# Making kv of two batches together, with each remainder tile's o right behind a kv, in a linear-attention and MLP kernel

## The chip, the cores and the metric

The kernel runs on one core of a Trainium2 chip. The metric is the device time of one execution in microseconds (us). Five engines work side by side and tell each other through semaphores: TensorE (matmuls; the profile writes PE, and PEld for its weight loads), VectorE (DVE), ScalarE (ACT), GpSimd (POOL) and SyncE (SP). In this kernel SP issues transposing transfers and stores, and POOL issues the loads that cast from float32 to bfloat16.

## The reference

All sizes are fixed: 8 batches, 8 heads, 576 positions, head size 64, model size 512, hidden size 2048.

```python
kv = np.einsum('bhsd,bhse->bhde', k, v)
out = np.einsum('bhsd,bhde->bhse', q, kv)
rms = np.sqrt(np.mean(out * out, axis=-1, keepdims=True) + 1e-06)
attn = out / rms * g_norm
x = attn.transpose(0, 2, 1, 3).reshape(B, S, H * D)
mu = np.mean(x, axis=-1, keepdims=True)
var = np.mean((x - mu) ** 2, axis=-1, keepdims=True)
xn = (x - mu) / np.sqrt(var + 1e-06) * g_ln
result = x + np.maximum(xn @ w_ch1, 0.0) @ w_ch2
```

The attention has no softmax: for each head a 64 x 64 matrix kv is made from k and v, and q is multiplied by it. Then come a norm per head, a layer norm over 512 columns, and two large matmuls with a ReLU between.

## The kernel before

**Tiles.** A batch's 576 positions are cut into four main tiles of 128 positions and a rest of 64. The rests of two neighbouring batches make one remainder tile: rem 1 holds those of batches 0 and 1, rem 3 of 2 and 3, rem 5 of 4 and 5, rem 7 of 6 and 7. The four remainder tiles form a block of their own, `"rem"`, which the MLP handles last.

**kv.** `kv_of(b)` makes kv of one batch: 40 matmuls with 64 weight columns each, for the head pairs alternately into the lower and the upper half of the array's columns. Two copies on ScalarE take it from PSUM into `kv_pack[b % 4]`. Batches 0 and 1 have code of their own near the start, the first with 64 rows as well.

**q.** `turn_q_dma(b)` copies q on VectorE into another order (`q_p`, line 203) and has SP transpose it by a transfer (`qt`, line 205).

**A tile** has four steps, recorded by `plan_tile`. `first`: `o` on TensorE (line 271: q times kv), its squares on ScalarE (277), their sum per head on VectorE (298). `second`: root (ACT, 308), reciprocal (315), `y` (303), `x` (322, 326) and `xc` (332) on VectorE. `third`: the variance on ScalarE (340). `fourth`: the transpose of `xc` into `xT_blk`, for batches from 2 on by a transfer on SP (352). A main tile's o is 4 matmuls with 128 weight columns, a remainder tile's o is 8 with 64, since each half of its rows has a kv of its own.

**The MLP** is the main stream: `mm1` (line 413), ReLU on ScalarE (416), `mm2` (429), `finish` on VectorE (434, writes `o_sb`), and two stores on SP (447, 448). It goes batch by batch, the remainder block last.

**The order is written by hand.** `mm1` and `mm2` call `tick()` after every few matmuls; each tick is a slot. From batch 3 on, batch b has slots 32 b to 32 b + 31: 16 of `mm1`, 16 of `mm2`, in each of them 4 matmuls of 512 columns. `at(slot, fn)` puts a function into a slot. All that a slot holds is recorded, in the order of its numbers, ahead of that slot's matmuls:

```python
    def tick():
        for _, fn in sorted(agenda.pop(clock[0], []), key=lambda e: e[0]):
            fn()
        clock[0] += 1
```

Every engine runs what is recorded for it strictly in this order; only the semaphores decide when. So a slot's number says where work stands in each queue and not when it starts.

**Slots before.** kv of batches 1, 2 and 3 in slots 22, 36 and 56; kv of 4 in 84, of 5 in 115, of 6 in 147, of 7 in 179. Remainder tiles: o in 62, 82, 146 and 210, with `second` two slots later. q of batch 3 in 56.7, of batch 4 in 84.7.

**Loads.** k, v and q each have two buffers (`NB = 2`), chosen by the batch's number. `load_batch(b, *after)` (lines 96 to 101) issues six transfers on POOL, two halves each for k, v and q. Ahead of them it copies one element of each tile in `after` into `gate`: POOL waits with the loads until that tile is there. Batch 4 waits for the transposed q of batch 3 and the last tile's `xT_blk` of batch 2, later batches for the transposed q of the batch before.

**PSUM.** `ps_out` has two buffers for o, `ps_m` one for kv and small transposes, `ps1` three for `mm1`, `ps2` two for `mm2`.

Of the kernel before, what the change touches and what calls it, by code (L numbers as in the profile page):

```python
# [14 lines left out]
def kernel(  # L15
# [11 lines left out]
    nc = tc.nc  # L27
    f32 = mybir.dt.float32
# [5 lines left out]
    B, H, S, D = q.shape  # L34
# [3 lines left out]
    nK = Dm // 128  # L38
    nDe = Dh // 128
    HP = H // 2  # L40
# [3 lines left out]
    J, JJ, JP = 4, 5, 9  # L44
    S_LO = 64 * JJ
    EPS = 1e-6
    NB = 2
# [8 lines left out]
    ps_m = ctx.enter_context(tc.psum_pool(name="ps_m", bufs=1))  # L56
# [15 lines left out]
    q_in = [consts.tile([128, H, JJ, D], bf16, name=f"q_in{i}") for i in range(NB)]  # L72
    k_in = [consts.tile([128, H, JJ, D], bf16, name=f"k_in{i}") for i in range(NB)]
    v_in = [consts.tile([128, H, JJ, D], bf16, name=f"v_in{i}") for i in range(NB)]
    kv_g = consts.tile([128, HP, 128], bf16)
    kv_pack = [consts.tile([128, HP, 128], bf16, name=f"kv_pack{i}") for i in range(4)]
# [9 lines left out]
    def lo(t, b, h0=0, h1=H):  # L86
        return t[b, h0:h1, :S_LO, :].rearrange("h (p j) d -> p h j d", j=JJ)

    def up(t, b, h0=0, h1=H):
        return t[b, h0:h1, S_LO:, :].rearrange("h (p j) d -> p h j d", j=J)  # L90

    def load(dst, t, b, h0=0, h1=H):
        nc.gpsimd.dma_start(dst[:64, h0:h1], lo(t, b, h0, h1))
        nc.gpsimd.dma_start(dst[64:, h0:h1, :J], up(t, b, h0, h1))

    def load_batch(b, *after):
        for element in after:
            nc.gpsimd.tensor_copy(gate, element)  # L98
        load(k_in[b % NB], k, b)
        load(v_in[b % NB], v, b)  # L100
        load(q_in[b % NB], q, b)

    def load_w1(c):
        n = Dh // 4
# [60 lines left out]
    qts, held, blks, rstds, m1s, q_ps = {}, {}, {}, {}, {}, {}  # L165
# [35 lines left out]
    def turn_q_dma(b):  # L201
        q_p = kv_in.tile([128, JJ, H, D], bf16, tag="qp", bufs=2)
        nc.vector.tensor_copy(q_p.rearrange("p j h d -> p h j d"), q_in[b % NB])
        q_t = qt_pool.tile([128, JJ, HP, 128], bf16, tag="qt", name="qt")
        nc.sync.dma_start_transpose(  # L205
            q_t.rearrange("p j hp t -> p (j hp) t"), q_p.rearrange("p j h d -> p (j h d)"))
        qts[b] = q_t
# [28 lines left out]
            nc.vector.tensor_mul(kv_g[D:, self.hps, D:], self.odd[D:], g[D:])  # L236
            del self.even, self.odd

    def kv_of(b):
        kv_ps = ps_m.tile([128, HP, D], f32, tag="misc", name="kv_ps")  # L240
        kvp = held[b] = kv_pack[b % 4]
        for hp in range(HP):
            for j in range(JJ):
                for hh in range(2):
                    h = 2 * hp + hh
                    nc.tensor.matmul(kv_ps[hh * D:hh * D + D, hp, :],  # L246
                                     lhsT=k_in[b % NB][:, h, j, :], rhs=v_in[b % NB][:, h, j, :],
                                     start=(j == 0), stop=(j == JJ - 1))
        nc.scalar.copy(kvp[:D, :, :D], kv_ps[:D])  # L249
        nc.scalar.copy(kvp[D:, :, D:], kv_ps[D:])  # L250

    def new_block(n, bufs):
        x_blk = xpool.tile([128, 4, Dm], f32, tag=f"x{n}", bufs=bufs, name="x_blk")
        st_blk = xpool.tile([128, 3, 4], f32, tag=f"st{n}", bufs=bufs, name="st_blk")
        xT_blk = xpool.tile([128, nK, 512], bf16, tag=f"xT{n}", bufs=bufs, name="xT_blk")
        return x_blk, st_blk, xT_blk
# [98 lines left out]
    def main_tile(b, j, pool=None, tag="ops"):  # L355
        q_t, kvp = qts[b], held[b]
        if b not in blks:
            blks[b] = new_block("main", 3)
        return Tile([(slice(0, 128), lambda hp: q_t[:, j, hp, :], kvp)], blks[b], j, pool, tag)

    def rem_tile(b):
        mms = []
        for half, bb in enumerate((b - 1, b)):
            qt, kp = qts.pop(bb), held.pop(bb)
            mms.append((slice(half * 64, (half + 1) * 64),
                        lambda hp, qt=qt: qt[:, J, hp, :64], kp))
        if "rem" not in blks:
            blks["rem"] = new_block("rem", 1)
        return Tile(mms, blks["rem"], b // 2)

    def plan_tile(s, make, turn_at, on_pe):
        box = []

        def first():
            t = make()
            box.append(t)
            t.o()
            t.sq()
            t.red()

        def second():
            t = box[0]
            t.y()
            t.x()
            t.xc()

        def third():
            box[0].var()

        def fourth():  # L390
            box[0].turn(on_pe)

        at(s, first)
        at(s + 2, second)
        at(s + 6, third)
        at(turn_at, fourth)

    def m1_of(b):
# [20 lines left out]
    def rstd_of(b):  # L419
        rstd = work.tile([128, 4], f32, tag="rstd", bufs=3, name="rstd")  # L420
        nc.scalar.activation(rstd, blks[b][1][:, 2, :], func=AF.Sqrt, scale=1.0 / Dm, bias=eps_sb)  # L421
        nc.vector.reciprocal(rstd, rstd)  # L422
        rstds[b] = rstd
# [45 lines left out]
    def at(slot, fn):  # L469
        agenda.setdefault(int(slot), []).append((slot, fn))  # L470
# [119 lines left out]
    def next_loads():  # L590
        nc.gpsimd.memset(k_in[0][64:, :, J], 0.0)
        nc.gpsimd.memset(v_in[0][64:, :, J], 0.0)
        load_batch(2)

    at(1, before_1)
    at(2, before_2)
    at(5, lambda: t[2].turn(True))
    at(5.1, before_5)
    at(9.5, next_loads)
    at(11, lambda: t[3].turn(True))  # L600
    for i in range(4):
# [17 lines left out]
    at(14.5, q_start)  # L619
    at(19, q_turns)  # L620
    at(22, lambda: kv_of(1))
    for j, s, tn in ((0, 24, 30), (1, 27, 34), (2, 31, 38), (3, 35, 42)):
        plan_tile(s, lambda j=j: main_tile(1, j), tn, True)
    at(46, lambda: rstd_of(1))

    at(36, lambda: kv_of(2))
    at(36.9, lambda: turn_q_dma(2))
    for j, s, tn in ((0, 45, 51), (1, 49, 55), (2, 53, 61), (3, 57.5, 64)):
        plan_tile(s, lambda j=j: main_tile(2, j), tn, False)
    plan_tile(62, lambda: rem_tile(1), 69, False)  # L630
    at(78, lambda: rstd_of(2))

    for b in range(3, B):
        s = 32 * b
        at(47 if b == 3 else s - 60,
           lambda b=b: load_batch(b, qts[b - 1][:1, J, HP - 1, 127:],
                                  *([blks[2][2][:1, nK - 1, 511:]] if b == 4 else [])))
        d = -41 if b == 3 else -45
        at(s + d + (1 if b < 5 else 0), lambda b=b: kv_of(b))
        at(s + d + 1.7, lambda b=b: turn_q_dma(b))  # L640
        for j in range(J):
            o = s + d + (11 if b == 3 else 13) + 5 * j
            plan_tile(o, lambda b=b, j=j: main_tile(b, j), o + 6, False)
        if b % 2:
            plan_tile(s - 14, lambda b=b: rem_tile(b), s - 8, False)
        at(s + 14, lambda b=b: rstd_of(b))
    at(32 * B + 14, lambda: rstd_of("rem"))


# [56 lines left out]
```

## Time and profile before

| What | us |
|---|---|
| Median of 3 runs (lowest, highest) | 291.13 (290.49, 291.29) |
| The profiled execution | 290.6 |
| Its span, first to last instruction | 288.8 |
| Large matmuls, lines 413 and 429, busy | 131.6 and 129.1 |
| The o of tiles, line 271, busy | 13.7 |
| kv of batches 1 to 7, line 246, busy | 5.8 |

Most matmuls have 512 columns. They overlap, so that the mean of one (379 ns) is longer than the distance from one start to the next. The page's second part shows the span in 40 equal slices, each digit a tenth of busy time:

```profile
PE   7889999999999999999999999999999999999994
PEld 3579756995479644444444444444444444444444
DVE  5774119938897783764376935762578200220022
ACT  3477844985379733872288318921893066016400
POOL 8522510041005004100500032000000000000000
PEclk9999999999999999999999999999999999999999
DMA  7999999979788959996994189947203410230033
```

One slice is 7.2 us. TensorE is busy all along, VectorE is nearly full in some slices between 58 and 108 us, and the DMA engines have full slices wherever loads run. The clock that TensorE was granted is full throughout.

The DMA issues of the page tell the sizes of the transfers and the median time from issue to landing:

```profile
out_dram<-o_sb SPq DMA_DIRECT2D x70, 128.0 KB, 2.4
...
q_in<-in_q_dram POOLq DMA_DIRECT2D x7, 320.0 KB, 12.3
k_in<-in_k_dram POOLq DMA_DIRECT2D x7, 320.0 KB, 6.0
v_in<-in_v_dram POOLq DMA_DIRECT2D x7, 320.0 KB, 8.6
```

A half of a tensor is 320 or 256 KB as it is written, in bfloat16.

### The profile page before, as it was taken

To read this page: it belongs to the slowest core of one execution; us is meant where nothing else is said; L and a number is where in the kernel's file an instruction comes from. 1 tells how busy PE (TensorE), PEld (TensorE's weight loads), DVE (VectorE), ACT (ScalarE), POOL (GpSimd) and SP (SyncE) were. 2 spreads that over 40 slices of the span, in tenths; PEclk is the share of its full clock that TensorE was granted. 3 is DMA by queue.
4 is the path that set the end of the run, shared out by engine and by line. 5 is a ranking of instruction groups with operands and counts; after the bars stand their busy time and mean duration, and the time that the engine had idled before them with its cause. 6 is when DMAs were issued, how large, how long until landed. Compare 5 with 4: busy or idle time off the path is not lost.

```text
span 288.8 us, 5753 instructions
## 1 busy us (share of the span) xinstructions
PE 280.9 (97%) x2295; PEld 157.9 (55%) x2295; DVE 149.8 (52%) x331; ACT 153.2 (53%) x333; POOL 41.0 (14%) x69
## 2 busy tenths in 40 slices
PE   7889999999999999999999999999999999999994
PEld 3579756995479644444444444444444444444444
DVE  5774119938897783764376935762578200220022
ACT  3477844985379733872288318921893066016400
POOL 8522510041005004100500032000000000000000
PEclk9999999999999999999999999999999999999999
DMA  7999999979788959996994189947203410230033
GB/s 214 199 206 205 198 190 195 214 112 193 138 173 101 194 108 157 202 159 120 157 217 68 39 152 219 155 84 149 56 18 64 101 36 0 48 81 19 0 73 75
DMA packets 67546, 36.76 MB, mean 127 GB/s; under 512 B 35516, under 2 KB 62524, under 8 KB 67520
## 3 DMA queue, kind: packets, MB, share of 16 engines
q0 software_dynamic: 28528, 17.76, 43.8%
q1 hardware_dynamic: 38480, 17.91, 31.2%
q10 hardware_dynamic: 512, 0.72, 0.7%
q8 instruction: 18, 0.29, 0.4%
q14 instruction: 8, 0.07, 0.1%
HBM read 36.71 MB, written 9.44 MB: 160 GB/s over the span
## 4 chain that ended last, share of the span: by engine, by line
PE 85%; DMA 5%; DVE 5%; ACT 2%; issue 1%; SPq 1%; DVEq 0%; POOLq 0%
PE p L413 41%; PE p L429 37%; PE o_ps L271 2%; DMA v_in<-in_v_dram 2%; DMA qt<-q_p 2%; PE kv_ps L246 2%; DMA xT_blk<-xc 1%; DVE ss L298 1%; ACT m L416 1%; DVE x_blk L322 1%; DVE y L303 1%; DVE o_sb L434 1%; PE p L198 1%; SPq L205 1%; ACT rms L308 0%
## 5 line engine op out<-in xcount | busy, mean ns | idle before, releaser
L413 PE MATMUL p<-xT_blk,w_sb 128*128 128x128 bf16 (+2 forms) x1024 | 131.6, 286 | 0.6 <-DMA xT_blk<-xc 0.2
L429 PE MATMUL p<-w_sb,m 128*128 128x512 bf16 (+2 forms) x608 | 129.1, 368 | 0.0
L416 ACT ACTIVATE m<-p 128x512 bf16<-128x512 f32 x144 | 85.2, 596 | 43.0 <-PE p L413 40.5
L413 PEld LDWEIGHTS <-w_sb 128*128 128x128 bf16 x1024 | 78.7, 98 | 44.9 <-issue 1.5
L429 PEld LDWEIGHTS <-m 128*128 128x128 bf16 x608 | 57.0, 98 | 62.0
L434 DVE SCALAR_TENSOR_TENSOR o_sb<-p,rstd,x_blk 128x512 f32<-128x512 f32 (+2 forms) x38 | 27.3, 720 | 52.2 <-PE p L429 41.2
L277 ACT ACTIVATE sq<-o_ps 128x512 f32<-128x512 f32 x35 | 20.9, 596 | 41.7 <-PE o_ps L271 41.7
L298 DVE TENSOR_REDUCE ss<-sq 128x8 f32<-128x512 f32 x35 | 23.7, 678 | 13.0 <-ACT sq L277 12.9
L340 ACT ACTIVATE dev<-x_blk,st_blk 128x512 f32<-128x512 f32 x36 | 25.7, 714 | 6.2 <-DVE st_blk L326 6.1
L332 DVE SCALAR_TENSOR_TENSOR xc<-x_blk,st_blk,g_ln_sb 128x512 bf16<-128x512 f32 x34 | 25.6, 752 | 1.2
L303 DVE TENSOR_TENSOR y<-o_ps,inv 128x512 f32<-128x512 f32 x33 | 22.8, 692 | 3.4 <-PE p L413 0.5
L322 DVE SCALAR_TENSOR_TENSOR x_blk<-y,g_norm_sb 128x512 f32<-128x512 f32 x33 | 22.8, 692 | 1.1
L315 DVE RECIPROCAL inv<-rms 128x8 f32<-128x8 f32 x36 | 7.2, 201 | 23.0 <-ACT rms L308 23.0
L422 DVE RECIPROCAL rstd<-rstd 128x4 f32<-128x4 f32 x9 | 1.6, 175 | 31.2 <-ACT rstd L421 31.1
L308 ACT ACTIVATE rms<-ss,eps_sb 128x8 f32<-128x8 f32 x36 | 10.7, 296 | 11.5 <-DVE ss L298 11.4
L98 POOL COPY gate<-qt 1x1 bf16<-1x1 bf16 x5 | 0.9, 177 | 106.4 <-DMA qt<-q_p 106.4
L271 PEld LDWEIGHTS <-qt 128*128 128x128 bf16 (+1 forms) x156 | 10.2, 100 | 8.1 <-issue 1.7
L271 PE MATMUL o_ps<-kv_pack,qt 128*128 128x128 bf16 (+1 forms) x156 | 13.7, 220 | 0.2
L198 PE MATMUL p<-fill_sb 128*128 128x512 bf16 x27 | 8.0, 448 | 1.2 <-DVE eps_sb L137 1.2
L340 ACT ACTIVATION_READ_ACCUMULATOR dev<-x_blk,st_blk 128x1 f32 x36 | 6.8, 189 | 0.0
L249 ACT CAST kv_pack<-kv_ps 64x256 bf16<-64x256 f32 x7 | 2.6, 366 | 7.7 <-PE kv_ps L246 7.7
L246 PEld LDWEIGHTS <-k_in 128*64 128x64 bf16 x280 | 5.0, 112 | 2.6 <-issue 2.5
(80 smaller groups left out, 110.5 us busy)
## 6 DMA issues: line engine op xcount, KB each, us to landing
out_dram<-o_sb SPq DMA_DIRECT2D x70, 128.0 KB, 2.4
w_sb<-in_moe_w_ch_dram POOLq DMA_DIRECT2D x8, 512.0 KB, 15.2
q_in<-in_q_dram POOLq DMA_DIRECT2D x7, 320.0 KB, 12.3
k_in<-in_k_dram POOLq DMA_DIRECT2D x7, 320.0 KB, 6.0
v_in<-in_v_dram POOLq DMA_DIRECT2D x7, 320.0 KB, 8.6
q_in<-in_q_dram POOLq DMA_DIRECT2D x8, 256.0 KB, 12.3
k_in<-in_k_dram POOLq DMA_DIRECT2D x7, 256.0 KB, 6.7
v_in<-in_v_dram POOLq DMA_DIRECT2D x7, 256.0 KB, 10.6
```

The source lines that it names most:

```text
L198: nc.tensor.matmul(p1, lhsT=fill_sb[:, :128], rhs=fill_sb, start=True, stop=True)
L271: nc.tensor.matmul(flat[rows, hp * 128:(hp + 1) * 128], lhsT=lhsT_of(hp), rhs=kvp[:, hp, :], start=True, stop=True)
L277: nc.scalar.activation(self.sq_t, self.o_ps, func=AF.Square)
L298: nc.vector.tensor_reduce(self.ss, self.sq_t, axis=AX.X, op=ALU.add)
L303: nc.vector.tensor_mul(self.y_t, self.o_ps, self.inv().to_broadcast([128, H, D]))
L322: nc.vector.scalar_tensor_tensor(x_blk[:, ts].rearrange("p (h d) -> p h d", h=H), in0=self.y_t, scalar=1.0, in1=g_norm_sb.to_broadcast([12 ...
L332: nc.vector.scalar_tensor_tensor(self.xc_t, in0=x_blk[:, self.ts], scalar=st[:, 1, self.ts:self.ts + 1], in1=g_ln_sb, op0=ALU.add, op1=ALU ...
L340: nc.scalar.activation(dev, x_blk[:, ts], func=AF.Square, bias=st[:, 1, ts:ts + 1], accum_out=st[:, 2, ts:ts + 1])
L413: nc.tensor.matmul(p1[:, i, :], lhsT=w1_sb[:, kk, de * 128:(de + 1) * 128], rhs=blk[2][:, kk, sl], start=(kk == 0), stop=(kk == nK - 1))
L416: nc.scalar.activation(m1[:, de0:de0 + per, sl], p1, func=AF.Relu)
L429: nc.tensor.matmul(p2[:, c0:c1], lhsT=m1s[b][:, de, ts * 128:(ts + 1) * 128], rhs=w2_sb[:, de, c0:c1], start=(de == 0), stop=(de == nDe - 1))
L434: nc.vector.scalar_tensor_tensor(o_sb[:, c0:c1], in0=p2[:, c0:c1], scalar=rstds[b][:, ts:ts + 1], in1=blks[b][0][:, ts, c0:c1], op0=ALU.mu ...
```

## The change

`kv_of` takes one batch or several. For two it makes 80 matmuls in a row into one PSUM tile of twice the size, and then four copies. It is called for (3), (4, 5) and (6, 7) in slots 56, 93 and 147. Right behind it, in the same slot, stands the o of a remainder tile: rem 1, rem 3 and rem 5. `plan_tile` has a new argument `x_at`, the slot of `second`. Rem 7 stays in slot 210.

The loads follow: `load_batches` takes a list of tensors. Behind the gate that let in k, v and q of batch 4 there stand now q, k and v of 4 and k and v of 5; the later gates let in q of one batch and k and v of the next. The order is q first.

Batch 3's tiles are planned 4.7 slots apart instead of 5, batch 4's q in slot 86.4 instead of 84.7, and batch 4's tiles from 97 in steps of 4.75 instead of from 96 in steps of 5. From batch 5 on, q and the main tiles stay in their slots.

```diff
-    def load_batch(b, *after):
+    def load_batches(what, *after):
         for element in after:
             nc.gpsimd.tensor_copy(gate, element)
-        load(k_in[b % NB], k, b)
-        load(v_in[b % NB], v, b)
-        load(q_in[b % NB], q, b)
+        tensors = {"k": (k_in, k), "v": (v_in, v), "q": (q_in, q)}
+        for name, b in what:
+            dst, src = tensors[name]
+            load(dst[b % NB], src, b)
...
-    def kv_of(b):
-        kv_ps = ps_m.tile([128, HP, D], f32, tag="misc", name="kv_ps")
-        kvp = held[b] = kv_pack[b % 4]
-        for hp in range(HP):
-            for j in range(JJ):
-                for hh in range(2):
-                    h = 2 * hp + hh
-                    nc.tensor.matmul(kv_ps[hh * D:hh * D + D, hp, :],
-                                     lhsT=k_in[b % NB][:, h, j, :], rhs=v_in[b % NB][:, h, j, :],
-                                     start=(j == 0), stop=(j == JJ - 1))
-        nc.scalar.copy(kvp[:D, :, :D], kv_ps[:D])
-        nc.scalar.copy(kvp[D:, :, D:], kv_ps[D:])
+    def kv_of(*bs):
+        kv_ps = ps_m.tile([128, len(bs), HP, D], f32, tag="misc", name="kv_ps")
+        for i, b in enumerate(bs):
+            for hp in range(HP):
+                for j in range(JJ):
+                    for hh in range(2):
+                        h = 2 * hp + hh
+                        nc.tensor.matmul(
+                            kv_ps[hh * D:hh * D + D, i, hp, :], lhsT=k_in[b % NB][:, h, j, :],
+                            rhs=v_in[b % NB][:, h, j, :], start=(j == 0), stop=(j == JJ - 1))
+        for i, b in enumerate(bs):
+            kvp = held[b] = kv_pack[b % 4]
+            nc.scalar.copy(kvp[:D, :, :D], kv_ps[:D, i])
+            nc.scalar.copy(kvp[D:, :, D:], kv_ps[D:, i])
...
-        at(s + 2, second)
-        at(s + 6, third)
+        at(x_at or s + 2, second)
+        at((x_at or s + 2) + 4, third)
...
-    plan_tile(62, lambda: rem_tile(1), 69, False)
...
-    for b in range(3, B):
-        s = 32 * b
-        at(47 if b == 3 else s - 60,
-           lambda b=b: load_batch(b, qts[b - 1][:1, J, HP - 1, 127:],
-                                  *([blks[2][2][:1, nK - 1, 511:]] if b == 4 else [])))
-        d = -41 if b == 3 else -45
-        at(s + d + (1 if b < 5 else 0), lambda b=b: kv_of(b))
-        at(s + d + 1.7, lambda b=b: turn_q_dma(b))
+    def turned_q(b):
+        return qts[b][:1, J, HP - 1, 127:]
+
+    at(47, lambda: load_batches((("k", 3), ("v", 3), ("q", 3)), turned_q(2)))
+    at(68, lambda: load_batches((("q", 4), ("k", 4), ("v", 4), ("k", 5), ("v", 5)),
+                                turned_q(3), blks[2][2][:1, nK - 1, 511:]))
+    at(100, lambda: load_batches((("q", 5), ("k", 6), ("v", 6)), turned_q(4)))
+    at(132, lambda: load_batches((("q", 6), ("k", 7), ("v", 7)), turned_q(5)))
+    at(164, lambda: load_batches((("q", 7),), turned_q(6)))
+
+
+    for s, bs, rem, x_at, tn in ((56, (3,), 1, 62, 69), (93, (4, 5), 3, 95, 101),
+                                 (147, (6, 7), 5, 149, 155)):
+        at(s, lambda bs=bs: kv_of(*bs))
+        plan_tile(s + .1, lambda rem=rem: rem_tile(rem), tn, False, x_at)
+    plan_tile(210, lambda: rem_tile(7), 216, False)
+
+
+    for b, at_q, at_o, step in ((3, 56.7, 66, 4.7), (4, 86.4, 97, 4.75),
+                                *((b, 32 * b - 43, 32 * b - 32, 5) for b in range(5, B))):
+        at(at_q, lambda b=b: turn_q_dma(b))
         for j in range(J):
-            o = s + d + (11 if b == 3 else 13) + 5 * j
+            o = at_o + step * j
             plan_tile(o, lambda b=b, j=j: main_tile(b, j), o + 6, False)
-        if b % 2:
-            plan_tile(s - 14, lambda b=b: rem_tile(b), s - 8, False)
-        at(s + 14, lambda b=b: rstd_of(b))
+        at(32 * b + 14, lambda b=b: rstd_of(b))
```

More of the change, by code (lines that the diff above doesn't have):

```diff
@@ L369, in rem_tile, with plan_tile @@
         return Tile(mms, blks["rem"], b // 2)
-    def plan_tile(s, make, turn_at, on_pe):
+    def plan_tile(s, make, turn_at, on_pe, x_at=None):
         box = []
@@ L592, in next_loads @@
         nc.gpsimd.memset(v_in[0][64:, :, J], 0.0)
-        load_batch(2)
+        load_batches((("k", 2), ("v", 2), ("q", 2)))
     at(1, before_1)
```

## The prediction

> **What bounds the kernel now.** I read the page's first two parts, then the chain of waits, then TensorE's own waits, then timelines of one stage. The page says that the matmul engine is all but full, and the chain says the same with one exception:
>
> ```profile
> PE 280.9 (97%) x2295; PEld 157.9 (55%) x2295; DVE 149.8 (52%) x331; ACT 153.2 (53%) x333; POOL 41.0 (14%) x69
> ...
> PE 85%; DMA 5%; DVE 5%; ACT 2%; issue 1%; SPq 1%; DVEq 0%; POOLq 0%
> ```
>
> So from some 20 us on a gain or loss must show in TensorE's stream. The stream has two kinds of hole. The first is around each phase with 64 weight columns (kv of a batch, or a remainder tile's o). TensorE's timeline around rem 5 and kv of batch 6:
>
> ```profile
> 157.19 0.81 PE L429 MATMUL p<-w_sb,m 128*128 128x512 bf16 x3
> 157.93 0.41 PE L271 MATMUL o_ps<-kv_pack,qt 128*64 128x128 bf16 x8
> 158.28 1.04 PE L429 MATMUL p<-w_sb,m 128*128 128x512 bf16 x4
> 159.24 0.82 PE L246 MATMUL kv_ps<-v_in,k_in 128*64 128x64 bf16 x40
> 160.00 1.25 PE L429 MATMUL p<-w_sb,m 128*128 128x512 bf16 x5
> ```
>
> Matmuls of 512 columns follow each other every 0.216 us (64 of them take 13.81 us late in the chain), so three from 157.19 end at 157.84, and o starts at 157.93: 0.09 us lost on entering. Its eight small matmuls run two abreast, four times 0.055 us, yet the next large one starts 0.35 us later: 0.13 lost on leaving. The second kind of hole is a late transfer, at 83.11 and between 108 and 112 us. The chain of waits there:
>
> ```profile
> 101.06 7.03 PE p L429 x32
> 108.08 1.55 SPq L205
> ...
> 109.69 2.52 DMA xT_blk<-xc
> ...
> 112.25 4.48 PE p L413 x20
> ```
>
> The transpose of the last tile of batch 3 stands on SP behind the large q transpose of batch 4 (issued 106.53, L205). Record by record TensorE loses 0.27 us at 111.14 (waiting for qt of batch 4), 0.39 at 111.80 (waiting for xT), and 0.21 at 82.79 (qt of batch 3).
>
> **What the skill says.** "TensorEngine Tiling (Array Packing)", Key Properties: changing the tiling mode, not merely the tile, drains TensorE. The trace agrees: 0.09 in and 0.11 to 0.12 out, at all eleven phases. "DMA: Bandwidth & Descriptors", Queues, rings and completion order: each DMA engine takes turns between queue rows, packet by packet. The trace agrees in kind: the first q transpose, issued at 32.30 among loads, took 14.4 us, the others about 5.0 alone. "TensorE: Matmul & The Clock Gate", Part 1: an idle window of about 3.4 us halves the clock. After the last matmul here (285.08) the recorded clock fell to one half 2.6 us later; no earlier idle stretch tests it.
>
> **Part 1, fewer phases.** Before: kv 1, 2, 3, rem 1, rem 3, kv 4, 5, rem 5, kv 6, 7, rem 7, eleven phases. The changed program's order on TensorE has kv 1, kv 2, kv 3 + rem 1, kv 4 + 5 + rem 3, kv 6 + 7 + rem 5, rem 7: six. Five removed, each 0.09 + 0.115 + 0.012 (the first large matmul after a phase is that much slower): 5 x 0.22 = -1.1 us. The seam from kv to rem inside a phase is nowhere in the trace; nothing to 0.06 us each, for three; I take nothing. Matmuls, copies and bytes are otherwise the same.
>
> **Part 2, rem 1 moves from slot 62 to 56.** A slot is one step of the main stream; slot 56 begins at 73.56, slot 66 at 83.34, slot 93 at 108.77. VectorE is full in this stage, and its order matters:
>
> ```profile
> 76.11 0.75 DVE L434 SCALAR_TENSOR_TENSOR o_sb<-p,rstd,x_blk 128x512 f32<-128x512 f32 x1
> 76.77 0.82 DVE L203 COPY q_p<-q_in 128x2560 bf16<-128x2560 bf16 x1
> ...
> 81.18 0.74 DVE L434 SCALAR_TENSOR_TENSOR o_sb<-p,rstd,x_blk 128x512 f32<-128x512 f32 x1
> ...
> 82.43 0.74 DVE L434 SCALAR_TENSOR_TENSOR o_sb<-p,rstd,x_blk 128x512 f32<-128x512 f32 x1
> ```
>
> The remainder's reduce (0.66 from start to start) now stands ahead of q_p of batch 3, which starts at 77.43. SP was busy with an output until 77.99, so its q transpose slips only from 78.09 to about 78.34, and qt lands at 83.3. Rem 1's y, x and xc (from slot 64 to 62) now pass the second o_sb, which moves from 82.43 to about 85.0 (rem's four steps take 2.6). On SP that output stands ahead of the transpose of batch 2's last tile, which slips from 85.71 to about 87.05 and lands at 89.6 instead of 88.3. Slot 72 needs it at 88.77. TensorE loses 0.25 to 0.4 at slot 66 and more at slot 72, in all about 1.1 us (0 to 1.4), and stands there at 89.65.
>
> **Part 3, batch 3 is planned a little earlier and q of batch 4 later (slots 84.7 to 86.4), rem 3 goes from slot 82 to 93.** On SP batch 3's last transpose now precedes the q transpose, and VectorE is rid of rem 3 (about 3.3 us) before it. Both holes at 111 us go: -0.66. What is late next is part 4.
>
> **Part 4, the loads.** POOL's timeline, and the landing times in a window of 90 to 104:
>
> ```profile
> 88.36 0.21 POOL L98 COPY gate<-xT_blk 1x1 bf16<-1x1 bf16 x1 [5.00 <-DMA xT_blk<-xc]
> 89.54 0.68 POOL L93 DMA_DIRECT2D k_in<-in_k_dram  x1 [0.97 <-PE p L413]
> ...
> 92.88 0.74 POOL L94 DMA_DIRECT2D q_in<-in_q_dram  x1
> ```
>
> ```profile
> k_in<-in_k_dram POOLq DMA_DIRECT2D x1, 320.0 KB, 5.2
> v_in<-in_v_dram POOLq DMA_DIRECT2D x1, 320.0 KB, 7.2
> q_in<-in_q_dram POOLq DMA_DIRECT2D x1, 320.0 KB, 9.4
> k_in<-in_k_dram POOLq DMA_DIRECT2D x1, 256.0 KB, 6.1
> v_in<-in_v_dram POOLq DMA_DIRECT2D x1, 256.0 KB, 8.1
> q_in<-in_q_dram POOLq DMA_DIRECT2D x1, 256.0 KB, 10.0
> ```
>
> Six halves of tensors land between 94.7 and 102.9: (102.9 - 94.7) / 5 = 1.63 us a half, at 194 to 200 GB/s in the windows 93 to 97, the rate also of the first loads at 27 to 50 us (195 GB/s), so the transfers are at their ceiling. The change puts ten halves behind the same gate: q, k, v of 4, then k, v of 5. kv of batch 5 stood at slot 115 (130 us) and its data had until then; now it stands in slot 93. The gate opens 1.3 us later (part 2), first issue about 90.8. Ten halves: 90.8 + 5.2 + 9 x 1.63 = 110.7 with nothing added. Beside them go, in the stretch 103 to 110, an output (256 KB, about 0.9 us), batch 3's last transpose (about 0.65, an estimate from the 0.13 MB it moves), and from 105.7 on the q transpose of batch 4, 5.0 us alone. If loads win the turns, v of 5 lands about 111; if the transpose takes its whole share, 116 to 117. I take 112.6.
>
> TensorE reaches kv of 4 at 108.77 + 0.88 (part 2 less the 0.22 already saved at kv 3) - 0.45 (rem 3 with its two edges) - 0.96 (kv 4 with its two edges) = 108.24, and kv of 5 at 109.0. The stream is in order, so it stands still 112.6 - 109.0 = 3.6 us (0 to 7.5); rem 3, the last tiles of mm2 for batch 2, and all of batch 3 stand behind it. That idle time may halve the clock: nothing, or up to 3.1 us at half speed (a start-up took from 1.2 to 4.3 us), which costs about 1.6; I take 0.5. Qt of 4 is needed at slot 97, 0.76 + 0.45 + 4 x 0.87 = 4.7 us after v of 5; it should be there by then. Later loads (k, v of 6; k, v of 7) have from 116 and from 139 to slot 147 (160 us), enough at 1.63 to 2.3 a half.
>
> **Sum.** -1.1 + 1.1 - 0.66 + 3.6 + 0.5 = +3.4. The profiled execution took 290.6 (span 288.8, 1.8 around it), within the three runs shown though 0.5 below their median: 290.6 + 3.4 = 294.0.
>
> **Rivals.** (a) The loads keep pace: v of 5 is in by about 109.5, because outputs and transposes find gaps; then -1.1 - 0.66 + 0.7 (half of part 2's estimate) = 289.5. For it: the page's slices reach 217 and 219 GB/s, above the 195 used here. Against: even the bare rate gives 110.7. (b) Near balance: v of 5 at 110.7, a wait of 1.7 and no clock loss: -1.1 + 1.1 - 0.66 + 1.7, 291.6. (c) Turns shared evenly: 116.5, a wait of 7.5, 1.6 of clock: 299.0; the 14.4 us transpose speaks for it. (d) The seam from kv to rem drains as well (0.6 back) so the change does little of what it says: 294.6 with the rest as forecast. The sign turns where v of 5 lands about 109.7, 0.7 us behind TensorE.
>
> **How the numbers follow.** Forecast 0.45; (a) 0.20; (b) 0.17; (c) 0.14; (d) 0.04. A measurement tells about 0.3%, 0.9 us, from no change. Faster: (a), 0.20. Within: most of (b), 0.13. Slower: the rest, 0.67. The range is 289.8 to 297.5: it leaves out part of (a) and nearly all of (c). The likeliest case's own range is 292.5 to 297.
>
> **What would show it.** Right: TensorE's waits name the load of v or k for kv around 109 to 113; the last of the ten halves lands 20 us or more after the gate; the holes at 111 us are gone; six phases, each with the old edges; slot 72 waits for xT. Wrong: kv of 5 starts without a wait, or the gate opens before 88.4, or the seam shows 0.1 us or more.

## The result, and the profile after

| | before | after |
|---|---|---|
| Median of 4 runs (lowest, highest), us | 290.81 (290.45, 291.29) | 300.01 (299.84, 300.73) |
| The profiled execution, us | 290.6 | 299.84 |
| Its span, us | 288.8 | 297.8 |
| Ratio after / before (95% interval) | | 1.032 (1.0295 to 1.0345) |

The change costs 9.2 us. The forecast was slower by 3.4: the sign and the place were right, the size was not, and 300.01 lies above the range given.

The page of the changed kernel, its first, second and fourth part. From here on, line numbers are those of the changed kernel: kv is L247, o L274, mm1 L416, mm2 L432, xT L355, qt L206. Ratios are to the kernel before, measured again beside each variant.

```profile
PE 281.2 (94%) x2295; PEld 158.6 (53%) x2295; DVE 149.7 (50%) x331; ACT 152.9 (51%) x333; POOL 40.9 (14%) x69
...
PE   7899999999997982999999999999999999999994
...
PEclk9999999999999996999999999999999999999999
...
PE 74%; DMA 17%; DVE 3%; ACT 2%; issue 1%; POOL 1%; DVEq 0%; POOLq 0%
```

TensorE has as many instructions as before and as many busy microseconds (281.2 against 280.9), so nothing was added to its work. Two slices have large holes, the 13th (89 to 97 us, a "7") and the 16th (112 to 119, a "2"; the hole begins in the 15th, an "8"). Only in the 16th is the clock below full. On the chain of waits DMA has gone from 5% to 17% of the span.

TensorE's own waits (total, how often, longest):

```profile
PE kv_ps L247 <- DMA v_in<-in_v_dram: 6.2, 1, 6.2
PE p L416 <- DMA xT_blk<-xc: 1.9, 1, 1.9
...
PE o_ps L274 <- DMA qt<-q_p: 0.6, 2, 0.4
```

The first line has no counterpart in the kernel before, and waits of the second kind were short there:

```profile
PE p L413 <- DMA xT_blk<-xc: 0.2, 1, 0.2
```

TensorE's timeline shows where the long one stands, and what comes after it:

```profile
104.75 5.34 PE L432 MATMUL p<-w_sb,m 128*128 128x512 bf16 x24
110.03 0.82 PE L247 MATMUL kv_ps<-v_in,k_in 128*64 128x64 bf16 x40
117.08 1.28 PE L247 MATMUL kv_ps<-v_in,k_in 128*64 128x64 bf16 x40 [6.23 <-DMA v_in<-in_v_dram]
118.13 0.66 PE L274 MATMUL o_ps<-kv_pack,qt 128*64 128x128 bf16 x8
118.72 3.40 PE L432 MATMUL p<-w_sb,m 128*128 128x512 bf16 x12
```

kv of 4 runs at 110.03, kv of 5 at 117.08. Behind the wait the same 40 matmuls take 1.28 us instead of 0.82, and the 8 of the remainder's o 0.66 instead of 0.41. That is the clock, as the windows show (length; busy time and instructions of PE, PEld, DVE, ACT, POOL; granted clock; DMA share; GB/s):

```profile
105.00:110.50 5.50, 5.50 (x54) 2.60 (x54) 1.54 (x3) 0.00 (x0) 0.00 (x0) 1.00 1.34 214
110.50:117.00 6.50, 0.35 (x23) 0.36 (x17) 0.00 (x0) 0.00 (x0) 0.00 (x0) 0.71 1.42 159
117.00:119.00 2.00, 1.92 (x49) 1.59 (x49) 0.00 (x0) 0.59 (x2) 0.13 (x1) 0.50 1.16 299
119.00:121.00 2.00, 2.00 (x8) 0.83 (x7) 0.43 (x1) 1.47 (x4) 1.66 (x4) 0.74 0.52 105
```

In the wait every compute engine stands still, and only the DMA engines work. Now the queue they work through. POOL's timeline (an issue's duration is that of its instruction, not of its transfer):

```profile
91.34 0.18 POOL L98 COPY gate<-xT_blk 1x1 bf16<-1x1 bf16 x1 [7.74 <-DMA xT_blk<-xc]
92.52 0.68 POOL L93 DMA_DIRECT2D q_in<-in_q_dram  x1 [1.01 <-DVE y L306]
...
98.94 0.68 POOL L94 DMA_DIRECT2D v_in<-in_v_dram  x1 [0.29 <-DMA q_in<-in_q_dram]
118.87 0.18 POOL L98 COPY gate<-qt 1x1 bf16<-1x1 bf16 x1 [19.25 <-DMA qt<-q_p]
```

The gate opens at 91.34 (88.36 before), and ten halves are issued from 92.52 to 98.94. The first lands at 97.09, the tenth, v of 5, at 117.04; kv of 5 starts 0.04 us later. The q transpose of batch 4, issued at 106.87, is there at 118.87: 12.0 us, where others alone took 5.0.

What shared the DMA engines with the loads, while the last nine halves landed (97.1 to 117.0):

```profile
q0 software_dynamic: 4544, 2.52, 105.8%
q1 hardware_dynamic: 3286, 1.04, 37.7%
```

And in the kernel before, while the last five of its six halves landed (94.7 to 102.9):

```profile
q0 software_dynamic: 2455, 1.35, 116.4%
q1 hardware_dynamic: 1106, 0.26, 20.3%
```

q0 holds the loads, q1 SP's stores and transposes; the columns are packets, MB, and the packets' time as a share of 16 engines' (packets overlap, so it can pass 100%). Before, loads had 84% of the bytes and came at 1.35 MB in 8.2 us, 165 GB/s. After, they have 71% and come at 2.52 MB in 19.9 us, 127 GB/s. A half took (117.04 - 97.09) / 9 = 2.2 us instead of 1.63.

Set against each other, matmul start by matmul start, the two traces give this account, where plus is lost:

| In TensorE's stream | us |
|---|---|
| Wait for v of 5 ahead of kv of 5 | +6.4 |
| Wait at slot 72 for xT of batch 2's last tile | +2.1 |
| Half clock, from kv of 5 to about 120.0 | +1.3 |
| o of batch 6's first tile waits for its qt (slot 160) | +0.4 |
| Slot 66, qt of batch 3: 0.53 instead of 0.21 | +0.3 |
| Two small delays elsewhere (38.5 and 86.1 us) | +0.3 |
| The two holes at 111 us, gone | -0.7 |
| Five phases fewer | -1.0 |
| Sum; the spans differ by 9.0 | +9.1 |

### The profile page after: what moved, and what is told of

Same layout as the page of the kernel before. It is cut to its first block, busy times and chain, and to the rows that moved or that the text cites. A ratio compares the mean times of both kernels' runs of the same rounds, so it can differ in the third digit from the quotient of the medians.

```text
span 297.8 us, 5755 instructions
## 1 busy us (share of the span) xinstructions
PE 281.2 (94%) x2295; PEld 158.6 (53%) x2295; DVE 149.7 (50%) x331; ACT 152.9 (51%) x333; POOL 40.9 (14%) x69
## 4 chain that ended last, share of the span: by engine, by line
PE 74%; DMA 17%; DVE 3%; ACT 2%; issue 1%; POOL 1%; DVEq 0%; POOLq 0%
PE p L416 37%; PE p L432 32%; DMA v_in<-in_v_dram 8%; DMA q_in<-in_q_dram 5%; DMA qt<-q_p 3%; PE o_ps L274 2%; PE kv_ps L247 1%; ACT m L419 1%; DVE x_blk L292 0%; DVE ss L301 0%; DVE o_sb L437 0%; POOL q_in L93 0%; ACT xT_blk L353 0%; ACT rms L311 0%; DVE xc L550 0%
## 5 line engine op out<-in xcount | busy, mean ns | idle before, releaser
L416 PE MATMUL p<-xT_blk,w_sb 128*128 128x128 bf16 (+2 forms) x1024 | 132.1, 286 | 2.3 <-DMA xT_blk<-xc 1.9
L432 PE MATMUL p<-w_sb,m 128*128 128x512 bf16 (+2 forms) x608 | 128.7, 369 | 0.0
L416 PEld LDWEIGHTS <-w_sb 128*128 128x128 bf16 x1024 | 78.5, 98 | 46.9 <-DMA xT_blk<-xc 2.2
L432 PEld LDWEIGHTS <-m 128*128 128x128 bf16 x608 | 57.5, 98 | 63.6 <-issue 1.0
L343 ACT ACTIVATE dev<-x_blk,st_blk 128x512 f32<-128x512 f32 x36 | 25.7, 714 | 12.2 <-DVE st_blk L329 12.2
L274 PE MATMUL o_ps<-kv_pack,qt 128*128 128x128 bf16 (+1 forms) x156 | 13.9, 224 | 0.6 <-DMA qt<-q_p 0.6
L274 PEld LDWEIGHTS <-qt 128*128 128x128 bf16 (+1 forms) x156 | 10.4, 103 | 7.1 <-DMA qt<-q_p 1.4
L247 PE MATMUL kv_ps<-v_in,k_in 128*64 128x64 bf16 x280 | 6.0, 203 | 6.3 <-DMA v_in<-in_v_dram 6.2
L247 PEld LDWEIGHTS <-k_in 128*64 128x64 bf16 x280 | 5.5, 119 | 8.1 <-issue 8.0
```

Source lines behind the costliest of these rows:

```text
L247: nc.tensor.matmul(kv_ps[hh * D:hh * D + D, i, hp, :], lhsT=k_in[b % NB][:, h, j, :], rhs=v_in[b % NB][:, h, j, :], start=(j == 0), stop=( ...
L274: nc.tensor.matmul(flat[rows, hp * 128:(hp + 1) * 128], lhsT=lhsT_of(hp), rhs=kvp[:, hp, :], start=True, stop=True)
L343: nc.scalar.activation(dev, x_blk[:, ts], func=AF.Square, bias=st[:, 1, ts:ts + 1], accum_out=st[:, 2, ts:ts + 1])
L416: nc.tensor.matmul(p1[:, i, :], lhsT=w1_sb[:, kk, de * 128:(de + 1) * 128], rhs=blk[2][:, kk, sl], start=(kk == 0), stop=(kk == nK - 1))
L432: nc.tensor.matmul(p2[:, c0:c1], lhsT=m1s[b][:, de, ts * 128:(ts + 1) * 128], rhs=w2_sb[:, de, c0:c1], start=(de == 0), stop=(de == nDe - 1))
```

## The experiments

The theory after the result: the loads of batch 5 are due 22 slots earlier than before (slot 93 instead of 115), and what the DMA engines have to move until then does not fit. Rival A: the gate opens too late, and an earlier one cures it. Rival B: it isn't the place of kv of 5 but the length of the queue behind the gate, so that another transfer is late when kv of 5 is moved back alone.

### kv of 5 back to slot 115, loads as changed

```diff
-    for s, bs, rem, x_at, tn in (..., (93, (4, 5), 3, 95, 101),
+    for s, bs, rem, x_at, tn in (..., (93, (4,), 3, 95, 101),
...
+    at(115, lambda: kv_of(5))
```

> The changed kernel (300.0), with kv of batch 5 alone moved back to slot 115; kv of 4 and rem 3 stay together in slot 93, and all loads stay as changed (ten halves behind one gate). Theory A, the wait is kv of 5 standing where its data is not there yet: the 6.4 us wait and the 1.1 us of half clock go, one phase (0.22) comes back: about 292.7. Rival B, the ten halves fill the DMA queues, whoever stands first: the transposed q of batch 4, which took 12.0 us from issue to landing, is now what TensorE waits for in slot 97, 3 to 4 us at about 114.5, and the time is about 296.

Measured: 296.24 (295.23 to 297.14), ratio 1.0189 (1.0156 to 1.0221). The wait is not gone, it has moved. TensorE's timeline of this kernel:

```profile
109.92 0.82 PE L247 MATMUL kv_ps<-v_in,k_in 128*64 128x64 bf16 x40
...
113.85 1.04 PE L416 MATMUL p<-xT_blk,w_sb 128*128 128x512 bf16 x4 [0.19 <-DMA xT_blk<-xc]
117.61 0.61 PE L274 MATMUL o_ps<-kv_pack,qt 128*128 128x128 bf16 x4 [2.72 <-DMA qt<-q_p]
```

kv of 4 and rem 3 pass. Then o of batch 4 (slot 97) waits 2.7 us for its qt, which was issued at 106.83 and took 10.7 us among the ten halves; its four matmuls take 0.61 us instead of 0.39, since the clock is at one half from 117.45 on. The trace is of one of the two slower executions (297.0 and 297.1; the others took 295.2 and 295.4), and what parts them is open. Rival B holds. A due time moved back relieves only its own waiter, while the queue stays as long.

### kv of 5 and its loads back

```diff
-    at(68, lambda: load_batches((("q", 4), ("k", 4), ("v", 4), ("k", 5), ("v", 5)),
+    at(68, lambda: load_batches((("q", 4), ("k", 4), ("v", 4)),
...
-    at(100, lambda: load_batches((("q", 5), ("k", 6), ("v", 6)), turned_q(4)))
+    at(100, lambda: load_batches((("k", 5), ("v", 5), ("q", 5), ("k", 6), ("v", 6)),
+                                 turned_q(4)))
```

with the two edits of the run above.

> As the run before, but k and v of 5 are loaded behind the next gate again (six halves behind the first gate: q, k, v of 4; then k, v, q of 5 and k, v of 6). Theories A and B: no wait at kv of 4 or 5, the q transpose of batch 4 takes about 5 us again, and what is left over before is rem 1 in slot 56 (2.4 us) less three phases saved (0.7) and less the 0.66 us of holes at 111 us: about 291.8. A rival by which the longer stretches of small matmuls or their copies cost something would leave 294 or more.

Measured: 292.41 (292.11 to 294.23), ratio 1.008 (1.005 to 1.0111). In the profiled execution nothing waits at kv of 4, kv of 5 or slot 97, and the clock is 1.000. (One of the four executions took 294.23 with a mean clock of 0.994; it has no trace.) Of the 9.2 us, 7.6 go with these edits. (The loads were not moved back with kv of 5 left in slot 93.) Beside those of the start, TensorE's waits have one large line left, that of slot 72:

```profile
PE p L416 <- DMA xT_blk<-xc: 2.0, 1, 2.0
```

### The gate without batch 2's last tile

```diff
-                                turned_q(3), blks[2][2][:1, nK - 1, 511:]))
+                                turned_q(3)))
```

> The changed kernel, with the ten halves waiting only for the transposed q of batch 3 (83.4 us) and no longer for the last transpose of batch 2 (91.3 us). If the start of the loads sets when kv of 5 can run: v of 5 lands about 7 us earlier, near 110, and the wait at kv of 5 falls from 6.4 to 1 or less and the clock stays full. Against it the loads now run beside the last two transposes of batch 2, which took 6 to 8 us among loads against 2.5 alone, so the wait in slot 72 grows from 2.1 to 4 to 7 us. Sum: 294 to 298. If the wait at kv of 5 stays above 4 us, it is not the start of the loads that sets it.

Measured: 299.38 (298.16 to 300.07), ratio 1.0303 (1.0275 to 1.0331). That is above the 294 to 298 expected. The loads go out from 84.21 instead of 92.52, and kv of 5 doesn't wait: kv of 4 and 5 are 80 matmuls in 1.46 us from 115.94. The transpose that the gate had kept ahead of them now runs among them. TensorE's timeline:

```profile
87.00 1.91 PE L416 MATMUL p<-xT_blk,w_sb 128*128 128x256 bf16 x16
95.58 4.39 PE L416 MATMUL p<-xT_blk,w_sb 128*128 128x256 bf16 x24 [6.67 <-DMA xT_blk<-xc]
```

6.7 us, with the half clock from 92.07 to 98.90: the same loss 22 us earlier. Rival A falls: the earlier gate cures the wait that it was meant for, and not the time. The gate protects a transfer that TensorE needs soon, and what it holds back is DMA time that has to be spent somewhere.

### Rem 1's second step back to 64

```diff
-    for s, bs, rem, x_at, tn in ((56, (3,), 1, 62, 69), ...
+    for s, bs, rem, x_at, tn in ((56, (3,), 1, 64, 69), ...
```

> The changed kernel with one number changed: the second step of rem 1 (y, x, xc) in slot 64 instead of 62, so behind the output step that it had passed on VectorE. Theory: on SP the transpose of batch 2's last tile is issued at about 85.8 instead of 87.05 and the 2.1 us wait in slot 72 goes nearly all; the wait of 0.5 us in slot 66 (rem 1's sum ahead of the copy of q) stays. The loads start about 3 us earlier, TensorE comes 2.1 earlier to kv of 5, so the wait there falls by about 0.9: 297.0. Rival: the slot 72 wait comes from rem 1's sum and o in slot 56, not from the output's place; then the time stays at 299.5 to 300.

Measured: 298.15 (297.85 to 298.96), ratio 1.0269 (1.0253 to 1.0286). The wait at slot 72 is gone altogether. Slot 66 still loses 0.52, so its loss doesn't come from the second step. TensorE arrives at kv of 5 earlier, but so do the loads, and the wait there stays:

```profile
114.35 1.28 PE L247 MATMUL kv_ps<-v_in,k_in 128*64 128x64 bf16 x40 [6.12 <-DMA v_in<-in_v_dram]
```

The expected gain was 3.0, the measured one 1.9. The wait shrank by 0.1 instead of 0.9, and the half clock behind it cost more: from the start of kv of 5 to slot 97 it took 6.9 us, in the changed kernel 5.7.

### The instruction packet moved

In the changed kernel the transpose for slot 72 was issued at 87.05, to the hundredth as forecast, but landed 4.2 us later instead of 2.6. TensorE's timeline:

```profile
91.27 0.94 PE L416 MATMUL p<-xT_blk,w_sb 128*128 128x256 bf16 x7 [1.91 <-DMA xT_blk<-xc]
```

The transpose's own 512 packets of 256 bytes had all started by 89.1. At 89.09 the trace has one packet of 16,384 bytes in queue q8, "instruction", for 1.08 us, and of the next transpose's 512 packets 27 come up to 0.6 us after the rest, about the share of one of 16 engines (32). So the completion of the first seems to have waited on the engine that fetched instructions; that is inferred, since the trace doesn't name engines. "Runtime: NRT & Kernel Launch", Instruction fetch mechanics, says that each engine's instructions are refilled in blocks of 16 KiB by a DMA queue of its own and that this is mostly hidden. The trace has such packets, 18 of 16 KB, between 0.9 and 1.5 us each; whether this one was hidden, the next run asks. To move them without touching the stage, 10 of the filler matmuls at the start (whose results nothing uses) were cut into 40 short ones: 30 more matmuls, each with its weight load, so 60 more TensorE instructions at almost the same length.

```diff
-    fill(18)
+    p1 = fill(8)
+    for _ in range(40):
+        nc.tensor.matmul(p1[:, :128], lhsT=fill_sb[:, :128], rhs=fill_sb[:, :128],
+                         start=True, stop=True)
+    del p1
```

> The changed kernel, with 10 of the 18 idle warm-up matmuls of 512 columns at the start made into 40 of 128 columns: the same array time (about 4.3 us at the clock of the start), 60 more instructions on TensorE, nothing else. In the changed kernel the last transpose of batch 2 is issued at 87.05 and lands only at 91.2, 4.2 us instead of 2.5, with one instruction packet of 16 KB (1.08 us) at 89.09 in its way. Theory: that packet is TensorE's own next stretch of code and holds up one of the 16 rings that the transpose needs. Sixty instructions are 30 matmuls of 0.109 us, so the packet comes 3.3 us earlier, before the transpose, which then lands at 89.6: the wait in slot 72 falls from 2.1 to 0.5 us and the time from 300.0 to about 298.5. Rival: the transpose is slow for the stores ahead of it and the next transpose behind it; then the wait stays at 2 us and the time at 300.

Measured: 298.86 (298.52 to 299.31), ratio 1.0283 (1.0269 to 1.0297). The packet now runs at 85.58. DMA queues from 89.0 to 90.2, the changed kernel:

```profile
q1 hardware_dynamic: 472, 0.11, 62.2%
q8 instruction: 1, 0.02, 5.6%
```

and the one with 60 more instructions:

```profile
q1 hardware_dynamic: 524, 0.13, 53.0%
```

TensorE's and then POOL's timeline of the latter:

```profile
89.67 2.58 PE L416 MATMUL p<-xT_blk,w_sb 128*128 128x256 bf16 x22 [0.50 <-DMA xT_blk<-xc]
```

```profile
89.75 0.18 POOL L98 COPY gate<-xT_blk 1x1 bf16<-1x1 bf16 x1 [6.31 <-DMA xT_blk<-xc]
```

Issued at 86.97, there by 89.7: 2.7 us. The wait at slot 72 is 0.5 by the timeline (0.67 between starts, 2.08 before), and the gate opens 1.6 us earlier. So of the 2.1 us at slot 72, 1.4 are this packet's meeting with the transpose, and 0.7 are the later issue that the forecast had. The whole gain is 1.15 us, since the half clock behind kv of 5 cost more here too (6.7 us from its start to slot 97). In the three other kernels with the same order ahead of slot 72 (kv of 5 back, with its loads or without, and the filled wait) the packet stands at 88.9 to 89.1 as well, and the wait there is 2.0 to 2.3.

### The wait filled with matmuls

28 matmuls of 512 columns, whose result nothing reads, between kv of 4 and kv of 5 in the changed kernel: the wait stays, but the array isn't idle.

```diff
         for i, b in enumerate(bs):
+            if b == 5:
+                fill(28, ps1.tile([128, 512], f32, tag="p1", name="dead"))
             for hp in range(HP):
```

> The changed kernel with 28 matmuls of 512 columns on zeros put between kv of 4 and kv of 5 (work that nothing uses, 28 x 0.216 = 6.05 us), into the wait for v of 5. If the clock's halving after the idle wait costs 1.1 us, and since two more phase edges cost 0.2: the clock stays full and the time is 300.0 - 0.9 = 299.1. If the slow stretch behind the wait has another cause (the loads' own traffic, PSUM), the time is 300.2 or more.

Measured: 298.34 (298.1 to 298.49), ratio 1.0261 (1.0246 to 1.0276). TensorE's timeline:

```profile
110.91 6.22 PE L199 MATMUL dead<-fill_sb 128*128 128x512 bf16 x28
117.05 0.82 PE L249 MATMUL kv_ps<-v_in,k_in 128*64 128x64 bf16 x40
117.71 0.39 PE L276 MATMUL o_ps<-kv_pack,qt 128*64 128x128 bf16 x8
```

(Lines stand two further down in this kernel.) kv of 5 starts at 117.05, as in the changed kernel at 117.08, but at full speed. The program is 1.7 us faster for 28 needless matmuls, where 0.9 was expected. From the start of kv of 5 to slot 97 it takes 4.45 us here and 5.74 in the changed kernel, so the traces put the cost of the half clock at 1.3; the two profiled executions differ by 1.35, so the rest of the 1.7 may be the spread of the executions. The loads run beside kv of 5 here too, so it isn't their traffic that slowed it.

### What is left of the idea: four phases fewer

kv of 5 and its loads back, and rem 1's second step at 64.

> Both costs undone together: kv of 5 and its loads back as in kv5_and_loads_back, and rem 1's second step in slot 64 as in rem1_x64. What stays of the change: kv 3 + rem 1, kv 4 + rem 3, kv 6 + 7 + rem 5. If the two causes are separate and complete, 292.4 - 2.1 (slot 72) = 290.3, that is before (290.5) less four phases (0.9) and the holes at 111 us (0.66), plus 0.35 more in slot 66 and 0.4 in slot 160 and what the early rem 1 leaves open. If a third cost is hidden in the change, 291 or more.

Measured: 289.92 (289.79 to 290.12, nine runs), the kernel before 290.65, ratio 0.9977 (0.9968 to 0.9986). TensorE's timeline has the phase kv of 4 with rem 3, without a wait:

```profile
107.75 0.82 PE L247 MATMUL kv_ps<-v_in,k_in 128*64 128x64 bf16 x40
108.40 0.39 PE L274 MATMUL o_ps<-kv_pack,qt 128*64 128x128 bf16 x8
108.73 1.47 PE L432 MATMUL p<-w_sb,m 128*128 128x512 bf16 x6
```

Four phases fewer and the two holes gone, 1.5 us, less 0.4 more at slot 66 and 0.4 at slot 160: 0.7, which is the difference of the spans (288.8 and 288.1).

### Further variants

The first of them is the same kernel with q of batch 3 ahead of rem 1's o (slot 56.05 instead of 56.7) and rem 5's second step in slot 151.

> As both_back, with the copy of q of batch 3 recorded ahead of rem 1's o (slot 56.05), and rem 5's second step in slot 151 so that the copy of q of batch 6 (slot 149) stands ahead of it. If the slot 66 wait comes from rem 1's sum standing ahead of that copy, it falls from 0.52 to 0.2 us; the 0.4 us in slot 160 goes. Sum: 289.6. If the order on VectorE is not what makes these waits, no change from both_back.

Measured: 289.75 (289.38 to 291.96), ratio 0.9982 (0.9967 to 0.9997). The wait at slot 160 is gone, so it was rem 5's second step that made it. At slot 66 the loss above the kernel before falls from 0.4 to 0.2. Ten of 14 executions took 289.4 to 290.1 and four 290.9 to 292.0. The profiled one is of the four: slot 72 waits 1.7 us again, an instruction packet at 88.26 beside the transpose issued at 86.12, which lands 4.2 us later. The other three have no trace. The same kernel with the 60 more instructions:

> The same shift in best2, whose executions lay in two groups (around 289.5 and around 291) and whose profile shows a wait of 1.7 us in slot 72 with the packet at 88.26. Theory: the second group goes, and the time is 289.4, all executions within half a microsecond. Rival: the two groups stay.

Measured: 290.48 (290.16 to 291.04), ratio 0.9994 (0.9986 to 1.0003): 1.1 us above the 289.4 expected, though the two groups are gone. The transpose took 2.7 us again, but it was issued at 87.18 instead of 86.12, since SP's store instruction ahead of it took 1.45 us instead of 0.54, with the packet, now at 85.12, beside it. Slot 72 waits 1.0. That the packet slowed the store's issue is what the times suggest; no run separates it.

The other way is to bring the remainder's o to a kv that keeps its place: rem 1 with kv of 4 in slot 84, rem 3 with kv of 5 in 115, rem 5 with kv of 6 and 7 in 147, o first, kv of 3 alone. The loads are those of "kv of 5 and its loads back". The lines that these replace are left out:

```diff
+    at(56, lambda: kv_of(3))
+    for s, bs, rem, x_at, tn in ((84, (4,), 1, 88, 94), (115, (5,), 3, 118, 124),
+                                 (147, (6, 7), 5, 151, 157)):
+        plan_tile(s, lambda rem=rem: rem_tile(rem), tn, False, x_at)
+        at(s + .05, lambda bs=bs: kv_of(*bs))
```

> Another way to save four phases: rem 1 with kv of 4 in slot 84, rem 3 with kv of 5 in 115, rem 5 with kv of 6 and 7 in 147 (its second step in 151), kv of 3 alone; loads as in kv5_and_loads_back. No kv moves ahead of where it was (but 7), so no load has to be earlier; rem 1 leaves the stage in which VectorE is full. Phases -0.9, holes at 111 us -0.66, slots 66 and 72 as before: 290.5 - 1.5 = 289.0. If saving phases were worth nothing, 289.9 or more.

Measured: 294.45 (294.36 to 295.49), ratio 1.0138 (1.0124 to 1.0152), where 289.0 was expected. The loads of batch 4 were left q first, so that v came third, and kv of 4 was now nine slots earlier than in the changed kernel:

```profile
103.24 1.22 PE L247 MATMUL kv_ps<-v_in,k_in 128*64 128x64 bf16 x40 [2.92 <-DMA v_in<-in_v_dram]
```

It is the fault of the change once more, in small: a due time moved, and the loads not asked. With k and v of 4 ahead of q, and slot 85:

> As best1, with k and v of 4 loaded ahead of q of 4 as in the kernel before, and rem 1 and kv of 4 one slot later (85). In best1 kv of 4 waited 3.1 us for v of 4, which stood third behind q, and the clock halved. Theory: both go (3.1 + 1.3 us): 290.0 at most, 289.4 if nothing else is late. Rival: the wait comes from the gate or from the transposes and stays above 2 us.

Measured: 289.57 (289.53 to 289.86), the kernel before 290.74, ratio 0.9965 (0.9952 to 0.9977), the lowest median of all. TensorE's timeline there:

```profile
100.60 0.41 PE L274 MATMUL o_ps<-kv_pack,qt 128*64 128x128 bf16 x8
100.85 0.80 PE L247 MATMUL kv_ps<-v_in,k_in 128*64 128x64 bf16 x40
101.81 9.44 PE L432 MATMUL p<-w_sb,m 128*128 128x512 bf16 x43 [0.16 <-issue]
```

Seven phases instead of eleven and no holes at 111 us, 1.5 less, and 0.5 more at slot 66, since TensorE comes there earlier and qt of batch 3 doesn't: 1.0 of the 1.1 by which the spans differ (288.8 and 287.7).

## Why the prediction was right or wrong

The mechanism was the forecast's: TensorE came to kv of 5 at 110.65 and waited for the load of v, the last of the ten halves landed 25.7 us after the gate, the holes at 111 us went, and slot 72 waited for xT. What failed are sizes, one of them above all: when v of 5 lands.

**Part 1, fewer phases: right.** The six phases keep their edges, 0.09 in and 0.11 to 0.12 out, and the seam from kv to rem shows 0.003 us. Five fewer gave 1.0 (forecast 1.1). Rival (d) is out.

**Part 2, rem 1 in slot 56: the order right, one term too small.** The q transpose of batch 3 was issued at 78.36 (forecast about 78.34) and landed at 83.31 (83.3), batch 2's last transpose was issued at 87.05 (87.05). The term that failed is "lands at 89.6": it took the 2.6 us of the kernel before, and measured 4.2, landing at 91.2. Slots 66 and 72 lost 2.4 together instead of 1.1. With the instruction packet elsewhere it is 1.0, so that the reading of the queues was good, and the 1.4 are a collision. The trace of before has the same packet at 89.20, inside the flight forecast for the transpose (87.05 to 89.6); but there the transpose had landed at 88.3, so nothing showed what such a packet costs.

**Part 3: right.** Both holes at 111 us are gone, 0.66. That qt of batch 4 was in time for slot 97, as forecast in part 4, was luck: TensorE stood still for v of 5. With that wait away, qt was 2.7 us late.

**Part 4: the step that failed is "I take 112.6".** v of 5 landed at 117.04. That the gate opened 1.7 us later than forecast explains none of the wait, since slot 72 delayed TensorE as much: it came to kv of 5 at 110.65 instead of 109.0. What is left is the distance from the first half to the tenth: 20.0 us measured, 9 x 1.63 + 1.9 = 16.6 forecast. The first half came 0.6 sooner after its issue than assumed, so the wait grew by 3.4 - 0.6 = 2.8, from 3.6 to 6.4. The mistake was to take 1.63 us a half, measured where loads had 84% of the bytes, for a stretch in which SP's queue moved 1.04 MB in 19.9 us (0.26 in 8.2 before) and the whole rate was 180 instead of 198 GB/s, to allow only 1.9 us for all that, and so to let the loads win most of the turns. The forecast had both ends, 111 and 116 to 117, and gave no reason for a value so near the first.

"DMA: Bandwidth & Descriptors", Queues, rings and completion order, which the forecast cited, says that the engines take turns packet by packet. The trace fits that: while the q transpose of batch 4 ran (106.9 to 116.9), 1,915 packets of loads started beside 2,095 of SP's queue (the trace's packets need not be the page's). Rival (c), turns shared evenly, fits: it had v of 5 at 116.5, which is 20.5 us after the first half against 20.0 measured, and 299.0 us. That its total came so close is partly luck: its wait of 7.5 us is 1.1 longer than the measured one and stands in for what slots 66 and 72 cost more. It was given 0.14, although the 14.4 us transpose stood in the profile; the q transposes of 12.0 us here and 10.7 in the first experiment are the same thing. The "ceiling" of 195 GB/s is not one for every mix of transfers: from 117 to 119 us the engines moved 299. In rival (a) half of part 2's 1.1 us is 0.55 and not 0.7, which changes its 289.5 to 289.4.

**The clock: the term too small.** 0.5 was taken; the trace shows 1.3 and the filled wait 1.7. "That idle time may halve the clock" came true in all six kernels here with a wait of 2.7 us or more that nothing filled. "TensorE: Matmul & The Clock Gate", Part 1, which the forecast cited, has an idle window of about 3.4 us. In the changed kernel the clock fell 2.6 us after the start of the last matmul ahead of the wait, in two others 4.2 and 4.8 us after it: there is no one length, and the last section shows the raster behind it.

**Not in the sum:** rem 5's second step in slot 149 makes qt of batch 6 late by 0.4 at slot 160, the small form of what part 2 saw for rem 1; and 0.3 in single delays.

Together: 3.4 forecast, 2.8 more at kv of 5, 1.3 at slots 66 and 72, 0.8 of clock, 0.7 not in the sum: 9.0.

The range ended at 297.5, short of (c). The sign was safe in all cases in which v of 5 came late, but a wait behind a full queue has no upper end near its middle: whoever gives the even sharing 0.14 leaves out a seventh of the chance on the expensive side.

## What to carry to other kernels

Moving work earlier moves the due time of all its data: add up what every queue must move until then, stores and transposes too, and price the loads at the share they get among those and not at the rate they had elsewhere. Before a load is held back or let in earlier, ask who is next in the queue: here moving the user alone and opening the gate alone each handed the wait to another transfer, and only moving the loads with their user took it away. A long wait of TensorE can cost its length and half clock on top: here waits of up to 2.3 us left the traced clock full, and all of 2.7 us and more halved it; behind the waits of about 6 us for v of 5 that cost 1.3 to 2.4 us, by where the wait lay (see the clock's raster below).

## What the runs showed of the hardware

The array's change to 64 weight columns and back cost 0.20 to 0.22 us a phase, and two kinds of work with the same tiling in a row cost nothing at their seam (0.003 us).

A transfer may be late through a packet that belongs to no transfer of the program, an instruction packet of 16 KB, about 1 us long: the transpose for slot 72 took 4.2 us with the packet beside it and 2.7 with the packet 3.5 us earlier. The packet moved when TensorE got 60 more instructions at the start, so it carries TensorE's, and these 30 harmless matmuls moved the kernel by 1.15 us.

The clock changes on a raster. In the changed kernel's trace it rises at 3.98, falls at 113.21, rises at 120.03 and falls at 297.53; the distances, 109.23, 6.83 and 177.49 us, are 32, 2 and 52 times 3.413. The half clock lasted 6.83 us (two steps) in the four kernels with a wait of about 6 us or more, and 3.41 (one step) in the two with 2.7 and 2.9.

Each step seems to set the clock of the next by how long TensorE was busy in it. In the changed kernel the step from 89.32, with the wait at slot 72, was 44% busy, and the clock stayed full; the step from 109.80 was 31% busy, and half clock followed. In the 13 traces every full-clock step with 44% or more was followed by full clock and every one with 34% or less by half. Back to full it took a busier step: 86% in the changed kernel, while 46% (60 more instructions) and 50% (second step at 64) left the clock at half. So the cost of a wait depends on where in the raster it lies. In these three kernels full clock came back at 120.03, 120.09 and 119.65, though kv of 5 started at 117.08, 115.10 and 114.35: the stretch of work at half speed grew from 3.0 to 5.0 and 5.3 us, and part of what was won ahead of it was lost again.
